# A state-space convolution beside attention on one core: the seeds' first loads, slots and powers rearranged

## The chip, the cores and the metric

The kernel runs on one core of a Trainium2 chip. A core has a matrix engine (TensorE, PE in the profile), three elementwise engines (VectorE or DVE, ScalarE or ACT, GpSimd or POOL), a queue engine that only issues transfers here (SyncE, SP) and 16 DMA engines that its queues share. The metric is the device time of one execution in microseconds; lower is better. All times below are in microseconds (us) unless marked ns.

## The reference, cut to what matters

Two independent halves are computed in float32 and put side by side. The first is a diagonal state-space layer: a kernel of 2048 taps per channel is built from 256 complex modes, and the input is convolved with it by FFT. The second is attention with 16 heads of width 28.

```python
dt = jnp.exp(log_dt)                                  # 448 channels
A = -jnp.exp(log_A_real) + 1j * A_imag                # 448 x 256 modes
C = (C_real + 1j * C_imag) * dt[:, None]
P = jnp.exp((A * dt[:, None])[:, :, None] * pos[None, None, :])   # pos = 0..2047
K = 2.0 * jnp.einsum("dn,dnl->dl", C, P).real
y = irfft(rfft(u_t, 2 * L) * rfft(K, 2 * L), 2 * L)[:, :, :L]  + u * D_skip
qkv = x @ wqkv                                        # 2048 x 448 @ 448 x 1344
p = softmax(q @ k.T * scale);  out_B = (p @ v) @ wo
```

## The kernel before, in words

The exponentials `P` are not computed one by one. For each mode only eleven powers are, those to the exponents 1, 2, 4, ... 1024 (`LV = 11`), and everything else is a product of them. The kernel has two parts in time.

**Part one** (lines 212 to 551, about the first 250 us) does two jobs side by side. `project` (line 522) works through 48 matrix products: for each of four chunks of 512 tokens, eight products that give q and k of four groups of heads (`qk_proj`) and four that give v (`v_proj`). Each product is twelve matmuls into one of three PSUM tiles `pm`. `evac` then splits the result into a high and a low part: ScalarE writes the high part `hl`, VectorE the low part, for the first two chunks ScalarE, VectorE and GpSimd also make the differences `kb` and `dhl`, and SyncE stores the tiles to DRAM. The weights are split in the same way at the start, out of tiles called `tri` that the seeds use later. A next product can run while up to two results wait for their split.

The other job is `seeds(o)` (line 313), run for eight blocks `o` of 56 channels each. Its stages are, in order: `load` (four transfers of 56 x 256 values into `nat`), `exp_a` and three products with the time step `dts`, the fourth product, `turn` (TensorE turns the four tables into one PSUM tile `pn`; ScalarE copies the real part to `tr`), `phases` (VectorE reduces the phase of one step; then eleven phases `r` are its product with the constants `pw2`; GpSimd makes the eleven real exponents `mg` as the product of `tr` with `pw2`), `reduce`, `sines` (ScalarE: two Sin and one Abs over 128 x 1232), `sizes` (ScalarE: one Exp over 128 x 1232) with `g_base`, then `places`, `factors`, `e_base`, `e3`, `g_first`, `e5`, `g_copies` (products on VectorE and GpSimd, copies on ScalarE), and last `put_g` and `put_e`, the transfers of 1456 KB and 896 KB to DRAM tensors `sd`. ScalarE holds Exp and Sin in different function tables, and a load of a table (`ACT_TABLE_LOAD`) stands between them.

The two jobs are dealt into slots (lines 504 to 540). A new seed begins every `SP = 4` slots; the 48 products are spread over `PW = 37` slots. Stage `i` of seed `o` is written in slot `4 o + i`, its load two slots ahead of the seed's first slot, so there are 41 slots. After the 37th slot the last loads of part one are written. In this part the written order is not the order of issue: a planner with its own costs orders the instructions of every engine and queue anew, from their dependencies, their place in the text and the time it expects them to be ready. A transfer also waits until the transfer eight places ahead of it in that plan has landed, since eight semaphores are used in turn.

Then come the maxima of the first query block (`max_mm(0, ...)`, lines 544 to 546): 64 matmuls, each followed by a pass of VectorE. They need `khat` (the keys of group 0, from DRAM; each quarter of its buffer holds the projection weights of one group of heads until that group's last product), `kdif`, and `qhat` (the first queries). `qhat` buffers are three, and the seeds' `se` tiles are taken from the same three.

**Part two** (from line 864) keeps the written order (`KEPT["a"]`): 256 steps of attention with the state-space work dealt between them. In the compiled programs its order on all five engines is the same before and after the change.

Of the kernel before, what the change touches and what calls it, by code (L numbers as in the profile page):

```python
# [18 lines left out]
D = 448  # L19
# [18 lines left out]
FL = {"s": 2, "f": 3}  # L38
S0, SP, SW, SD, PW, E3 = 0, 4, 0, 5, 37, 8
UG = (2, 2, 4)  # L40
# [50 lines left out]
def body(ctx, tc, a, out):  # L91
# [120 lines left out]
    with ExitStack() as st:  # L212
# [18 lines left out]
        load_x(0)  # L231
        w_g = k0_t[:CK].rearrange("p g (i s k h e) -> p i s k g h e", i=2, s=2, k=NCK, h=HG)
        vh = y_p.tile([CK, NCK, D], F32R, name="vh")
        vl = y_p.tile([CK, NCK, D], F32R, name="vl")
        nc.gpsimd.memset(k0_t[:CK].rearrange("p g (n e) -> p (g n) e", e=32)[:, :, DH:].bitcast(F32), 0.0)
        vst = [x_p.tile([128, H, 32], F32, name=f"vst{i}") for i in range(2)]
        for t in vst:
            nc.gpsimd.memset(t[:, :, DH:DH + 1], 1.0)
            nc.gpsimd.memset(t[:, :, DH + 1:], 0.0)
        wns = []  # L240
        for i in range(2):
            wn = t_p.tile([128, 3, LV, BO * 16], F32, name="tri", bufs=2).rearrange("p t k h -> p (t k h)")
            wn = wn[:CK, :2 * 3 * D].rearrange("p (k s d) -> p k s d", k=2, s=3)
            wns += [wn[:, 0], wn[:, 1]]
        for k in range(NCK):
            nc.sync.dma_start(wns[k], wqkv[k * CK:(k + 1) * CK, :].rearrange("p (s d) -> p s d", s=3))
# [5 lines left out]
        def load_nat(o):  # L252
            nats[o] = s_p.tile([PO, 4, 256], F32, name="nat", bufs=2)
            for i, n in enumerate(("A_log_A_real", "A_A_imag", "A_C_real", "A_C_imag")):
                nc.sync.dma_start(nats[o][:, i, :], bass.AP(tensor=a[n].tensor, offset=a[n].offset + first(o) * 256,
                                                            ap=[[256, JF // 4], [JF * 256, 4], [1, 256]]))

# [3 lines left out]
        for f in range(2):  # L261
            nc.sync.dma_start(ldt[4 * f:4 * f + 4, :].rearrange("o (j i) -> o j i", j=4), bass.AP(
                tensor=t.tensor, offset=t.offset + f * DF, ap=[[JF // 4, 4], [JF, 4], [1, JF // 4]]))
        load_nat(0)
        pw2 = s_p.tile([128, LV], F32, name="pw2")
        nc.sync.dma_start(pw2, a["pw2"])
        half_pi = s_p.tile([128, 1], F32, name="half_pi")
        nc.gpsimd.memset(half_pi, TWO_PI / 4)
        nc.sync.dma_start(sel, a["sel"])
        nc.sync.dma_start(w1, a["w1"])  # L270
        for k in range(NCK):
            for s in (1, 0):
                src = wns[k][:, s, :].rearrange("p (g h e) -> p g h e", g=G, e=DH)
                hi, lo = (w_g[:, i, s, k, :, :, :DH] for i in range(2))
                nc.scalar.activation(hi, src, AF.Copy)
                nc.vector.tensor_tensor(lo, src, hi.bitcast(F32), ALU.subtract)
            nc.scalar.activation(vh[:, k, :], wns[k][:, 2, :], AF.Copy)
            nc.gpsimd.tensor_tensor(vl[:, k, :], wns[k][:, 2, :], vh[:, k, :].bitcast(F32), ALU.subtract)

# [24 lines left out]
        def turn_dt():  # L304
            dt_ps = ps_t.tile([128, CQ], F32, name="pt")[:PO, :NO]
            nc.tensor.transpose(dt_ps, dt_o, ident[:NO, :NO])
            for i, f in enumerate((1.0, 0.15915494309189535, 2.0, -2.0, -1.0)):
                nc.vector.tensor_scalar(dt_all[:, i, :], dt_ps, f, None, op0=ALU.mult)

        NH = BO * 16  # L310
        mul = lambda e, o_, x_, y_: e.tensor_tensor(o_, x_, y_, ALU.mult)

        def seeds(o):
# [6 lines left out]
            vk = lambda t, k: t[:, k:k + 3, :].rearrange("p k (b h) -> p k b h", h=16)  # L320

            def exp_a():
                act.activation(q["nat"][:, 0, :], q["nat"][:, 0, :], AF.Exp)

# [4 lines left out]
            def turn():  # L329
                q["ps"] = ps = ps_n.tile([128, CQ], F32, name="pn")[:, :8 * PO].rearrange("p (a b h e) -> p a b h e", a=4, h=2, e=8)  # L330
                for i in range(4):
                    for h in range(2):
                        nc.tensor.transpose(ps[:, i, :, h, :], q["nat"][:, i, h * 128:(h + 1) * 128], ident[:PO, :PO])
                q["tr"] = s_p.tile([128, NH], F32, name="tr", bufs=2)
                act.activation(q["tr"], ps[:, 0].rearrange("p b h e -> p (b h e)"), AF.Copy)

            def phases():
                tri = t_p.tile([128, 3, LV, NH], F32, name="tri", bufs=2)
                q["r"], q["sn"], q["mg"] = r, sn, mg = tri[:, 0], tri[:, 1], tri[:, 2]
                t0, k0, im = sn[:, 0, :], sn[:, 1, :], q["ps"][:, 1].rearrange("p b h e -> p (b h e)")  # L340
                vec.tensor_scalar(k0, im, MAGIC, None, op0=ALU.add)
                vec.scalar_tensor_tensor(t0, k0, MAGIC, im, op0=ALU.subtract, op1=ALU.subtract)
                vec.tensor_scalar(t0, t0, 0.5, -0.5, op0=ALU.min, op1=ALU.max)
                mul(vec, r, lb(t0), kb)
                mul(pol, mg, lb(q["tr"]), kb)

            def reduce():
                vec.tensor_scalar(q["sn"], q["r"], MAGIC, MAGIC, op0=ALU.add, op1=ALU.subtract)
                vec.tensor_tensor(q["r"], q["sn"], q["r"], ALU.subtract)

            def sines():
                act.activation(q["sn"], q["r"], AF.Sin, scale=TWO_PI)
                act.activation(q["r"], q["r"], AF.Abs)
                act.activation(q["r"], q["r"], AF.Sin, scale=-TWO_PI, bias=half_pi)

            def sizes():
                act.activation(q["mg"], q["mg"], AF.Exp)

# [68 lines left out]
            def load():  # L427
                if o not in nats:
# [701 lines left out]
```

## Time and profile before

| | |
|---|---|
| runs (us) | 1301.16, 1301.76, 1304.81; median 1301.76 |
| profiled execution | span 1301.1 from the first to the last instruction; the page gives no other time for it |
| busy over the span | PE 94%, DVE 73%, ACT 73%, POOL 67% |
| granted TensorE clock, mean | 0.978 of full speed |
| bytes moved | 205.35 MB, 158 GB/s in the mean |

A row of the groups names line, engine, operation and tiles (`out<-in`), then how often it ran, the busy time in all, and the mean of one in ns. Nearly every instruction shows line 75, a helper that records them, so tiles tell them apart. A row of the timeline gives start, duration, engine, operation, how many were merged, and in brackets the idle time of the engine just before, with what ended it. A row of the table by stretches gives the length of the stretch, the busy time and count for each of PE, PEld (weight loads), DVE, ACT and POOL, the granted clock, the share of the DMA engines that was busy, and GB/s. SPq is the queue engine.

### The profile page before, as it was taken

How to read it: one execution, taken by the hardware profiler on the slowest of the kernel's cores; microseconds unless marked ns; L12 is line 12 of the kernel's file. 1: busy time of each engine (PE TensorE's matmuls, PEld its weight loads, DVE VectorE, ACT ScalarE, POOL GpSimd, SP SyncE). 2: the span in 40 equal slices, each digit the busy share in tenths (PEclk: the TensorE clock that was granted, in tenths of full speed). 3: DMA queues.
4: the chain of work that ended last, by engine and by line, in shares of the span. 5: the costliest groups of instructions: out<-in, count | busy, mean ns of one | idle time of the engine just before them, and what ended most of it. 6: DMA issues, size and time to landing. Idle time of an engine off the chain costs nothing.

```text
span 1301.1 us, 33177 instructions
## 1 busy us (share of the span) xinstructions
PE 1228.2 (94%) x12625; PEld 701.0 (54%) x12625; DVE 948.0 (73%) x2106; ACT 952.4 (73%) x2068; POOL 871.1 (67%) x736
## 2 busy tenths in 40 slices
PE   6878985899999999999999999999999999999997
PEld 5657763355555555555555555555555555544433
DVE  5887896987777887787788888888888655645111
ACT  4775763488888888888888888888887766756552
POOL 3676683298888878888869999998996212424421
PEclk9888997999999999999999999999999999999999
DMA  6677769835866555458644131733425453647656
GB/s 194 203 258 244 249 206 294 237 77 124 195 137 149 124 146 148 140 147 231 181 126 96 54 95 32 182 91 83 103 51 148 153 158 133 201 144 244 198 162 174
DMA packets 200088, 205.35 MB, mean 158 GB/s; under 512 B 95993, under 2 KB 158521, under 8 KB 197881
## 3 DMA queue, kind: packets, MB, share of 16 engines
q1 hardware_dynamic: 199928, 203.23, 56.2%
q8 instruction: 100, 1.64, 0.5%
q14 instruction: 60, 0.48, 0.1%
HBM read 120.73 MB, written 82.18 MB: 156 GB/s over the span
## 4 chain that ended last, share of the span: by engine, by line
PE 71%; DVE 10%; DMA 6%; POOL 5%; ACT 3%; issue 3%; SPq 0%; POOLq 0%; ACTq 0%; DVEq 0%
PE pm L75 40%; PE pss L75 16%; PE po L75 15%; DVE tri L75 2%; DVE mx L75 2%; POOL e L75 1%; POOL qhat L75 1%; DMA k<-hl 1%; ACT tri L75 1%; DVE qhat L75 1%; DVE sg L75 1%; DMA tri<-in_B_wqkv 1%; DVE px L75 1%; DMA khat<-k 1%; DMA ut<-in_A_u 1%
## 5 line engine op out<-in xcount | busy, mean ns | idle before, releaser
L75 ACT ACTIVATE p<-pss 128x512 f32<-128x512 f32 x1024 | 560.9, 609 | 111.6 <-PE pss L75 108.6
L75 PE MATMUL pss<-qhat,khat 128*128 128x512 f32 x1024 | 402.5, 399 | 1.5 <-ACT p L75 1.4
L75 DVE TENSOR_REDUCE mx<-pm 128x1 f32<-128x512 f32 x500 | 321.4, 684 | 109.2 <-PE pm L75 107.1
L75 PE MATMUL pm<-khat,qhat 128*128 128x512 f32 x749 | 326.3, 438 | 3.4 <-DVE mx L75 2.1
L75 POOL TENSOR_TENSOR e<-e,sdb 128x256 f32<-128x256 f32 x168 | 202.0, 1202 | 116.2 <-ACT e L75 61.2
L75 PE MATMUL po<-p,v 128*32 128x512 f32 x2048 | 269.1, 594 | 0.0
L75 POOL TENSOR_TENSOR e<-e,eu 128x256 f32<-128x256 f32 x168 | 248.4, 1478 | 13.2
L75 PEld LDWEIGHTS pm<-khat,qhat 128*128 128x128 f32 x749 | 141.0, 189 | 199.7 <-ACT p L75 47.8
L75 DVE CUSTOM_DVE_ANT_0 rl<-pm,rl 128x512 f32<-128x512 f32 x249 | 171.4, 688 | 65.2 <-ACT rl L75 61.5
L75 PEld LDWEIGHTS pss<-qhat,khat 128*128 128x128 f32 x1024 | 190.2, 188 | 45.7 <-issue 10.8
L75 POOL TENSOR_TENSOR eu<-e,sdb 128x256 f32<-128x256 f32 x168 | 202.2, 1203 | 0.0
L75 POOL TENSOR_TENSOR p<-pr,pr 64x448 f32<-64x448 f32 x64 | 73.3, 1145 | 158.5 <-PE pm L75 133.2
L75 ACT ACTIVATE rl<-pm 128x512 f32<-128x512 f32 x249 | 150.8, 606 | 20.4 <-PE pm L75 20.4
L75 DVE TENSOR_TENSOR g<-g,zg 128x128 f32<-128x128 f32 x392 | 162.1, 413 | 3.4
L75 PE MATMUL pm<-xh,khat 112*128 112x512 f32 x256 | 94.1, 451 | 23.2 <-DVE hl L75 11.1
L75 PE MATMUL pm<-kdif,qhat 128*128 128x512 f32 x249 | 100.5, 404 | 2.6 <-DMA v<-v 1.3
L75 DVE TENSOR_TENSOR zg<-g,zg 128x128 f32<-128x128 f32 x224 | 88.0, 393 | 5.0
L75 PEld LDWEIGHTS pm<-e,g 128*32 128x32 f32 x3584 | 57.2, 109 | 43.8 <-issue 16.1
L75 DVE TENSOR_TENSOR pr<-pm,ub 128x448 f32<-128x448 f32 x64 | 37.0, 619 | 56.4 <-PE pm L75 42.0
L75 PEld LDWEIGHTS pm<-xh,khat 112*128 112x128 f32 x256 | 54.2, 217 | 39.4 <-DVE hl L75 12.9
L75 PE MATMUL pm<-e,g 128*32 128x64 f32 x3584 | 73.0, 222 | 1.9 <-POOL e L75 1.9
L75 ACT ACTIVATE y<-pm 128x448 f32<-128x448 f32 x48 | 26.5, 553 | 58.2 <-PE pm L75 33.8
(134 smaller groups left out, 1470.3 us busy)
## 6 DMA issues: line engine op xcount, KB each, us to landing
sdb<-sd SPq DMA_DIRECT2D x56, 336.0 KB
khat<-k SPq DMA_DIRECT2D x64, 256.0 KB
qhat<-q SPq DMA_DIRECT2D x64, 256.0 KB
sd<-sg SPq DMA_DIRECT2D x8, 1456.0 KB
k<-hl SPq DMA_DIRECT2D x16, 512.0 KB
q<-hl SPq DMA_DIRECT2D x16, 512.0 KB
mw<-in_mw SPq DMA_DIRECT2D x16, 512.0 KB
sd<-qhat SPq DMA_DIRECT2D x8, 896.0 KB
```

Source lines behind the costliest of these rows:

```text
L75: i = f(*args, **kw)
```

## The change

Four things change, all in part one.

1. The first seed's parameters (`ldt`, two transfers, and `nat`, four) are written ahead of the first rows of `x` and the weights, and are issued from ScalarE's queue instead of SyncE's. `exact_exp`, the time step's exponential in small VectorE steps, is written there too; `turn_dt` moves from the second slot to the first, and `pw2` is loaded ahead of `kones`.
2. Every stage of every seed is written three slots sooner (`SH = 3`), the loads too: stage `i` of seed `o` in slot `4 o + i - 3`. There are 38 slots; the products stay spread over 37.
3. The reduced phase is written back into the PSUM tile `pn` instead of into `tri`, and VectorE's eleven-fold product reads it from there. ScalarE's copy `tr` is gone.
4. GpSimd's product for `mg` is gone, and so is the one Exp over 128 x 1232. Instead ScalarE takes eleven exponentials of 128 x 112 straight from `pn`, with the factor 2^k as its scale, in the stage of `phases`, three stages sooner than `sizes` was. A chain `in_order` ties `exp_a`, `sizes` and `sines` of all seeds to be issued on ScalarE in the order in which they are written.

```diff
-S0, SP, SW, SD, PW, E3 = 0, 4, 0, 5, 37, 8
+SP, SH, PW, E3 = 4, 3, 37, 8
...
+        def load_nat(o, queue=nc.sync):
...
+            nc.scalar.dma_start(ldt[4 * f:4 * f + 4, :].rearrange("o (j i) -> o j i", j=4), bass.AP(
+                tensor=t.tensor, offset=t.offset + f * DF, ap=[[JF // 4, 4], [JF, 4], [1, JF // 4]]))
+        load_nat(0, nc.scalar)
...
         load_x(0)
...
-        nc.sync.dma_start(kones, a["kones"])
...
-        load_nat(0)
         pw2 = s_p.tile([128, LV], F32, name="pw2")
         nc.sync.dma_start(pw2, a["pw2"])
+        nc.sync.dma_start(kones, a["kones"])
...
+        table = []
...
+            def in_order(f):
+                def call():
+                    with tc.issue_after(table[0]) if table else nullcontext():
+                        i = f()
+                    table[:] = [i.ins]
+                return call
...
-                q["tr"] = s_p.tile([128, NH], F32, name="tr", bufs=2)
-                act.activation(q["tr"], ps[:, 0].rearrange("p b h e -> p (b h e)"), AF.Copy)
...
-                t0, k0, im = sn[:, 0, :], sn[:, 1, :], q["ps"][:, 1].rearrange("p b h e -> p (b h e)")
-                vec.tensor_scalar(k0, im, MAGIC, None, op0=ALU.add)
-                vec.scalar_tensor_tensor(t0, k0, MAGIC, im, op0=ALU.subtract, op1=ALU.subtract)
+                k0, (tr, t0) = sn[:, 1, :], (q["ps"][:, i].rearrange("p b h e -> p (b h e)") for i in range(2))
+                vec.tensor_scalar(k0, t0, MAGIC, None, op0=ALU.add)
+                vec.scalar_tensor_tensor(t0, k0, MAGIC, t0, op0=ALU.subtract, op1=ALU.subtract)
                 vec.tensor_scalar(t0, t0, 0.5, -0.5, op0=ALU.min, op1=ALU.max)
                 mul(vec, r, lb(t0), kb)
-                mul(pol, mg, lb(q["tr"]), kb)
+                q["tr"] = tr
+
+            @in_order
+            def sizes():
+                return [act.activation(q["mg"][:, k, :], q["tr"], AF.Exp, scale=float(2 ** k)) for k in range(LV)][-1]
...
-            def sizes():
-                act.activation(q["mg"], q["mg"], AF.Exp)
...
-            return [[load], [exp_a] + dts(1, 2, 3), dts(0), [turn], [phases], [reduce], [sines], [sizes, g_base],
+            return [[load], [exp_a] + dts(1, 2, 3), dts(0), [turn], [phases, sizes], [reduce], [sines], [g_base],
                     [places, fa, e_base], [e3, g_first], [fb, e5, g_copies], [put_g], [put_e]]
...
-        n_stage = SP * (NO - 1) + len(stages[0])
+        n_stage = SP * (NO - 1) + len(stages[0]) - SH
...
-                slots[max(SP * o + (i or -2), 0)] += st_
-        slots[1].insert(0, turn_dt)
+                slots[max(SP * o + (i - SH if i else -2 - SH), 0)] += st_
+        slots[0].insert(1, turn_dt)
```

More of the change, by code (lines that the diff above doesn't have):

```diff
@@ L1 @@
 import collections
-from contextlib import ExitStack
+from contextlib import ExitStack, nullcontext
 import concourse.bass as bass
@@ L229, in load_x @@
                 nc.sync.dma_start(xns[c, h], xs[:, 2 * h:2 * h + 2, :])
[L231 to L246, printed above, removed]
[L247 removed]
         first = lambda o: (o // 4) * DF + (o % 4) * (JF // 4)
         nats = {}
[L252 removed]
+        def load_nat(o, queue=nc.sync):
             nats[o] = s_p.tile([PO, 4, 256], F32, name="nat", bufs=2)
             for i, n in enumerate(("A_log_A_real", "A_A_imag", "A_C_real", "A_C_imag")):
[L255 to L256 removed]
+                queue.dma_start(nats[o][:, i, :], bass.AP(tensor=a[n].tensor, offset=a[n].offset + first(o) * 256,
+                                                          ap=[[256, JF // 4], [JF * 256, 4], [1, 256]]))
         dt_all = s_p.tile([PO, 5, NO], F32, name="dt_all")
```

47 lines of the change are left out of this document (32 added, 15 removed).

## The prediction

> **What bounds the kernel now.** I read the table by stretches first, because the change touches part one alone. Part two issues in one order in both programs, so what part one saves or loses is passed on one for one, as long as part two starts from the same state.
>
> ```profile
> 0.00:200.00 200.00, 162.10 (x694) 129.06 (x695) 158.07 (x275) 136.86 (x270) 128.76 (x152) 0.91 0.69 227
> 0.00:20.00 20.00, 12.08 (x43) 9.17 (x44) 8.07 (x12) 9.26 (x17) 7.30 (x20) 1.00 0.78 214
> 80.00:100.00 20.00, 12.73 (x36) 9.79 (x37) 18.20 (x27) 17.59 (x31) 13.77 (x17) 0.68 0.65 228
> 200.00:220.00 20.00, 8.04 (x25) 5.55 (x24) 10.73 (x26) 4.03 (x9) 6.17 (x6) 0.67 1.03 296
> 220.00:240.00 20.00, 16.46 (x43) 7.45 (x43) 18.74 (x42) 6.58 (x11) 0.00 (x0) 0.99 1.05 279
> ```
>
> To be read: no engine is full in the first 200 us (TensorE 162.1, VectorE 158.1). TensorE has gaps and its granted clock falls with them (0.68 from 80 to 100, where 36 matmuls take 12.73 us). From 200 on the DMA engines are full (1.03, 1.05) and from 220 VectorE, with 18.74 of 20, makes the maxima. So part one has three limits in turn: TensorE's waits, then transfers, then VectorE. Next, TensorE's waits to 215 us:
>
> ```profile
> PE pm L75 <- DVE hl L75: 13.5, 7, 5.4
> PE pt L75 <- DMA qhat<-q: 12.0, 1, 12.0
> PE pm L75 <- DVE kb L75: 6.8, 4, 4.3
> PE pt L75 <- DVE xl L75: 6.1, 4, 2.8
> ```
>
> It waits 26.4 us for VectorE's splits (13.5 + 6.8 + 6.1) and 12.0 for the first queries. The largest wait, followed backwards from GpSimd's product for the powers:
>
> ```profile
> 77.02 3.44 POOL L75 TENSOR_TENSOR tri<-tr,pw 128x1232 f32<-128x1232 f32 x1
> ```
>
> ```profile
> 80.50 1.23 ACT L75 ACTIVATE tri<-tri 128x1232 f32<-128x1232 f32 x1 [2.79 <-POOL tri L75]
> 81.64 0.58 ACT L75 ACTIVATE hl<-pm 128x512 fp32r<-128x512 f32 x1
> ```
>
> ```profile
> 82.25 0.69 DVE L75 TENSOR_TENSOR hl<-pm,hl 128x512 fp32r<-128x512 f32 x1 [1.12 <-ACT hl L75]
> ```
>
> ```profile
> 83.00 2.08 PE L75 MATMUL pm<-xh,khat 112*128 112x512 f32 x4 [5.38 <-DVE hl L75]
> ```
>
> The Exp on ScalarE waits 2.79 us for that product. Behind it stands `hl` of a finished matrix product, behind that VectorE's half, and TensorE stands 5.38 us with all three PSUM tiles full. Its next four matmuls take 2.08. In all ScalarE waits for that product so often:
>
> ```profile
> ACT tri L75 <- POOL tri L75: 10.8, 4, 3.0
> ```
>
> The product also holds VectorE:
>
> ```profile
> 46.20 2.42 POOL L75 TENSOR_TENSOR tri<-tr,pw 128x1232 f32<-128x1232 f32 x1
> ```
>
> ```profile
> 46.92 1.77 DVE L75 TENSOR_SCALAR tri<-tri 128x112 f32<-128x112 f32 x1
> ```
>
> ```profile
> 49.35 0.47 PE L75 MATMUL pm<-vh,xh 112*128 112x448 f32 x1 [1.37 <-DVE hl L75]
> ```
>
> ```profile
> 86.52 0.22 DVE L75 TENSOR_SCALAR tri<-tri 128x112 f32<-128x112 f32 x1
> 86.77 1.44 DVE L75 TENSOR_TENSOR tri<-tri,pw 128x1232 f32<-128x1232 f32 x1
> ```
>
> A 128 x 112 operation that takes 0.22 alone took 1.77 and ended with GpSimd's product (46.20 + 2.42 = 48.62, 46.92 + 1.77 = 48.69). VectorE's split came after it, and TensorE lost 1.37. VectorE's own eleven-fold product took 1.44 where GpSimd was idle.
>
> The end of part one is a queue of transfers:
>
> ```profile
> 199.90 1.61 SPq L75 DMA_DIRECT2D qhat<-q  x2
> 202.10 0.50 SPq L75 DMA_DIRECT2D sd<-sg  x1
> 214.87 0.77 PE L75 MATMUL pt<-kdif,qhat 128*128 128x512 f32 x1 [11.96 <-DMA qhat<-q]
> ```
>
> ```profile
> sd<-sg SPq DMA_DIRECT2D x8, 1456.0 KB
> ```
>
> TensorE has been done for 11.96 us when the queries arrive. Between the two halves of their load stands a 1456 KB transfer of the seventh seed.
>
> **The change, part by part.** The durations:
>
> ```profile
> L75 ACT ACTIVATE tri<-tri 128x1232 f32<-128x1232 f32 x24 | 29.6, 1234 | 15.7 <-POOL tri L75 10.8 <-DVE tri L75 4.8
> ...
> L75 POOL TENSOR_TENSOR tri<-tr,pw 128x1232 f32<-128x1232 f32 x8 | 19.4, 2419 | 14.3 <-ACT tr L75 8.5 <-issue 5.8
> L75 ACT ACT_TABLE_LOAD x15 | 19.2, 1283 | 1.0 <-PEq L1120 0.7
> ...
> L75 DVE TENSOR_TENSOR tri<-tri,pw 128x1232 f32<-128x1232 f32 x8 | 15.1, 1886 | 0.1
> ...
> L75 DVE TENSOR_SCALAR tri<-tri 128x112 f32<-128x112 f32 x8 | 8.0, 1003 | 0.1
> ...
> L75 ACT ACTIVATE tr<-pn 128x112 f32<-128x112 f32 x8 | 2.2, 271 | 1.1 <-PE pn L75 0.9
> ```
>
> *Powers.* GpSimd loses 8 products of 2.419, 19.4 us. ScalarE loses 8 Exp of 1.234 and 8 copies of 0.271, and gets 88 exponentials of 128 x 112. One alone should take the 0.271 of the copy, which has the same source and shape; in a row they overlap:
>
> ```profile
> 195.35 1.22 ACT L75 ACTIVATE sg<-sg 128x112 f32<-128x112 f32 x6
> ```
>
> Six take 1.22, or 0.2 each, so eleven take 0.27 + 10 x 0.2 = 2.3 (at most 11 x 0.271 = 3.0). ScalarE pays 8 x (2.3 - 1.23 - 0.27) = +6.4, at most +12. The tied order makes 17 table loads of 15: two times 1.283 is +2.6. Together +9, and the 10.8 us of waits for GpSimd go: ScalarE is about even. The page "ScalarE: Activation LUTs" of the Trainium skill (section "What ACT_TABLE_LOAD costs") speaks against this: a switch of tables should cost about 2.66, a load of 1.283 and a drain of 1.38. By that rule the two loads would cost 5.3 and ScalarE's sum would be +11.7. The trace does not agree:
>
> ```profile
> 36.50 1.28 ACT L75 ACT_TABLE_LOAD   x1
> 37.79 1.23 ACT L75 ACTIVATE tri<-tri 128x1232 f32<-128x1232 f32 x1
> ```
>
> The Sin starts 0.01 after the load's end (36.50 + 1.28 = 37.78), so I keep 1.283 and +9.
>
> On the path: the waits of TensorE that follow from GpSimd's product are 5.38 and 1.37. I count both as gone, -6.75. The slow clock behind the larger comes on top. At the full clock two matmuls take 0.63:
>
> ```profile
> 36.91 0.63 PE L75 MATMUL pm<-xh,khat 112*128 112x512 f32 x2
> ```
>
> The 36 matmuls from 80 to 100 would then take 11.3 (18 x 0.63) and not 12.73: -1.4. What is late next at that place is VectorE's own `reduce`, also ahead of the split. The last of ScalarE's waits for GpSimd falls among the transfers of the end and is not counted twice.
>
> *Phases in PSUM.* The 128 x 112 step should take about 0.27 instead of 1.003, and cannot be held as above: -5.9 on VectorE. The eleven-fold product is bounded by 1.886 (no gain) and 1.44 (never held), -3.6. The page "SBUF — State Buffer" of the Trainium skill ("Who interferes with whom") says that two SBUF inputs, or a two-port mode, make VectorE and GpSimd exclude each other, and one input from PSUM does not. By that rule all 3.6 would come; the held and the free row above agree, but no run yet has the PSUM form. Of these 5.9 to 9.5 us little is on TensorE's path; its 12.9 us of waits for `kb` and `xl` come from VectorE's backlog. VectorE was busy 158.1 of the first 200 us, so a relief of 8 is a twentieth; I take twice that share of 12.9, -1.3, with 0 and half of it, -6.5, as ends.
>
> *Parameters first.* Six transfers move to ScalarE's queue and their 229 KB ahead of the weights.
>
> ```profile
> 1.20 0.93 SPq L75 DMA_DIRECT2D xn<-in_B_x  x2
> 2.17 1.94 SPq L75 DMA_DIRECT2D tri<-in_B_wqkv  x4
> ...
> 4.73 0.77 SPq L75 DMA_DIRECT2D ldt<-in_A_log_dt  x2
> 6.23 1.02 SPq L75 DMA_DIRECT2D nat<-in_A_log_A_real  x1
> ```
>
> ```profile
> 0.73 1.28 ACT L75 ACT_TABLE_LOAD   x1 [0.73 <-PEq L1120]
> 6.97 0.60 ACT L75 ACTIVATE xh<-pt 112x512 fp32r<-112x512 f32 x1 [4.96 <-PE pt L75]
> ```
>
> The issue costs 0.77 for `ldt` and about 1.0 for each of four `nat`, so about 4.8 us on ScalarE ahead of its table load: 0.73 + 4.8 + 1.28 = 6.8, and its first split was at 6.97 after 4.96 of idle time. That gap hides it; without it, it would cost the 4.8. On SyncE the weights' four issues now wait for `ldt`, the first rows of `x` and one `nat` to land, through the eight semaphores in turn (`nat` at 6.23 shows such a wait). Transfers of `x` are under way until then, so I charge only the bytes: 229 KB at 214 GB/s is +1.1; at worst nothing is under way and the weights start at 6.97, when the first rows have been turned, instead of 2.17: +4.8. The time step's small VectorE operations now fall in the idle start; TensorE's listed waits name none of them, so 0.
>
> *Three slots sooner.* By the plans, the seeds' order against the products moves by about two products at the end (the last Sin stood behind three of the last eight `hl`, and stands behind two). All later stages of a seed move, with their four loads and two `put` transfers on SyncE. No work goes. The seventh seed's 1456 KB now stand ahead of the first `khat` load, and the sixth seed's 2352 KB no longer fall among the last eight products: 1456 KB fewer are moved between the start of those products and the queries. At the 296 GB/s of the row from 200 to 220 that is 1456 / 296 = -4.9. If the transfers ahead have not drained, 0. The eighth seed's `put_g` still comes before three quarters of `khat`; these are needed one after another, and the maxima (VectorE 18.74 of 20 from 220) cover them.
>
> *New order.* The seeds' work now presses on ScalarE and VectorE sooner, and eleven exponentials stand in a block ahead of a split, where one Exp of 1.23 stood. Two of the three PSUM tiles cover a block of 2.3; where all are full it costs 2.3. I charge one such block, +2.3 (none to all eight, 18.4).
>
> Sum: -6.75 - 1.4 - 1.3 + 1.1 - 4.9 + 2.3 = -11.0. The span becomes 1301.1 - 11.0 = 1290.1; the median of the runs lies 0.7 above the span, so 1290.8.
>
> **The rivals.**
>
> *Slower: ScalarE's tied order.* Each seed's Sin must now wait for the next seed's `exp_a` and for its own eleven exponentials, and every split behind them waits too. For it: ScalarE is busy 17.59 of 20 us from 80 to 100, the stretch with the worst clock. Against it: the waits for GpSimd that it replaces are as long. Without the charge the sum is -13.3, so it decides from the sixth block of 2.3 on that meets full PSUM tiles: with all eight, +18.4 instead of +2.3, the sum is +5.1, and the time 1306.9.
>
> *No change at the end.* The transfers, full from 200 us, set when the queries arrive, and TensorE's gain turns into a longer wait for them (11.96 now). For it: shares of 1.03 and 1.05. Against it: SyncE had room before, with a share of 0.65 from 80 to 100. Then the gains ahead of it and the -4.9 vanish; with +1.1 the time is 1302.9.
>
> *More than the forecast.* The waits for `kb` and `xl` (12.9) are also offspring of GpSimd's product, and the clock stays up. For it: VectorE's rows held by it. Then half of 12.9 goes (-6.5 in place of -1.3) and no block is charged: -11.0 - 5.2 - 2.3 = -18.5, and 1283.3.
>
> **How the numbers follow.** Within 0.3% (3.9 us) of 1301.8 is about what a measurement cannot tell from no change. Forecast (1286 to 1297): 0.45. More: 0.20. No change at the end: 0.13, of which 0.04 keeps a gain of over 3.9. ScalarE's order: 0.19, of which 0.04 ends within 0.3%. The rest, 0.03, is a start that loses its 4.8 with no gain behind it. Faster: 0.45 + 0.20 + 0.04 = 0.69; same: 0.09 + 0.04 = 0.13; slower: 0.15 + 0.03 = 0.18. The range of eight in ten goes from 1280, beyond the third rival, to 1307, the first; the forecast's own range is 1286 to 1297.
>
> **What would show it.** ScalarE has no wait for GpSimd at `tri`, the eleven exponentials take 2.3 a block, table loads are 17; the 128 x 112 step on `pn` takes under 0.3 and the product on `pn` about 1.44; the largest wait of TensorE for `hl` is under 3; the queries arrive about 11 us sooner, and maxima and part two follow unchanged. Wrong it would be if waits of ScalarE for VectorE's `phases` took the place of those for GpSimd, or if TensorE ended sooner and the queries did not.

## The result, and the profile after

The changed kernel takes 1295.20 us (median of 1294.08 to 1295.62) against 1303.28 (1301.16 to 1305.12) for the kernel before on the same chip: a ratio of 0.993, with an interval of 0.9912 to 0.9948. It is 8.1 us faster; 11.0 were forecast. Its profiled execution took 1295.62, with a span of 1293.7 (before 1301.1).

The table by stretches of the changed kernel (length, then PE, PEld, DVE, ACT and POOL busy, granted clock, share of the DMA engines, GB/s):

```profile
0.00:20.00 20.00, 11.95 (x40) 8.66 (x41) 11.49 (x38) 10.86 (x22) 6.76 (x20) 1.00 0.87 237
...
80.00:100.00 20.00, 12.70 (x44) 9.69 (x43) 17.84 (x35) 16.74 (x41) 14.27 (x19) 0.83 0.72 249
...
200.00:220.00 20.00, 12.16 (x31) 6.66 (x31) 13.15 (x29) 5.56 (x10) 0.00 (x0) 0.71 1.05 288
220.00:240.00 20.00, 15.27 (x37) 7.60 (x38) 18.23 (x41) 5.46 (x10) 0.00 (x0) 0.89 0.81 214
0.00:200.00 200.00, 162.01 (x705) 127.77 (x705) 143.79 (x288) 142.17 (x348) 109.12 (x150) 0.94 0.74 245
```

Over 200 us VectorE does 143.79 instead of 158.07, GpSimd 109.12 instead of 128.76, ScalarE 142.17 instead of 136.86. From 80 to 100 the clock is 0.83 and no longer 0.68. From 200 to 220 the DMA engines are as full as before (1.05 for 1.03), from 220 to 240 they are less so (0.81 for 1.05). TensorE's waits up to 235 us:

```profile
PE pt L75 <- DMA khat<-k: 12.6, 1, 12.6
PE pm L75 <- DVE kb L75: 11.0, 5, 3.7
PE pm L75 <- DVE hl L75: 6.7, 5, 1.8
...
PE pt L75 <- DVE xl L75: 2.7, 2, 2.4
```

The waits for `hl` have halved (13.5 before), those for `xl` have more than halved (6.1), but those for `kb` have grown from 6.8 to 11.0. The wait of the maxima's first matmul is still there: 12.6, was 12.0, now put down to the keys (`khat`) and no longer to the queries. The groups of ScalarE and VectorE up to 215 us, and one block of exponentials in the timeline:

```profile
L75 ACT ACT_TABLE_LOAD x17 | 21.8, 1283 | 10.0 <-issue 5.1 <-DVE tri L75 4.7
...
L75 ACT ACTIVATE tri<-pn 128x112 f32<-128x112 f32 x88 | 15.1, 311 | 1.6 <-DVE tri L75 1.5
```

```profile
L75 DVE TENSOR_TENSOR tri<-pn,pw 128x1232 f32<-128x1232 f32 x8 | 11.4, 1430 | 0.0
...
L75 DVE TENSOR_SCALAR pn<-pn 128x112 f32<-128x112 f32 x8 | 2.3, 283 | 0.1
```

```profile
84.94 1.28 ACT L75 ACT_TABLE_LOAD   x1
86.23 1.83 ACT L75 ACTIVATE tri<-pn 128x112 f32<-128x112 f32 x11
```

A block of eleven takes 1.83, the table loads are 17, and no wait of ScalarE for GpSimd at `tri` is left. The end of part one, on the queue engine and then on TensorE:

```profile
190.95 2.53 SPq L75 DMA_DIRECT2D khat<-k  x4
...
194.33 1.45 SPq L75 DMA_DIRECT2D qhat<-q  x2
195.90 0.49 SPq L75 DMA_DIRECT2D q<-hl  x1
196.43 1.10 SPq L75 DMA_DIRECT2D qhat<-q  x2
```

```profile
206.56 0.76 PE L75 MATMUL pt<-kdif,qhat 128*128 128x512 f32 x1 [12.63 <-DMA khat<-k]
```

The row of the kernel before that answers to the first of these:

```profile
196.57 1.80 SPq L75 DMA_DIRECT2D khat<-k  x4
```

The load of the first keys is issued 5.6 us sooner (190.95 for 196.57), and from that issue to the maxima's first matmul 15.6 us pass instead of 18.3 (206.56 - 190.95; 214.87 - 196.57). Together that is 8.3, and from there to the end both kernels take about the same: 1293.7 - 206.56 = 1087.1 and 1301.1 - 214.87 = 1086.2. So the whole gain is made before the maxima.

### The profile page after: what moved, and what is told of

It is laid out like the page before. It is cut to its first block, busy times and chain, and to the rows that moved or that the text cites. A ratio compares the mean times of both kernels' runs of the same rounds, so it can differ in the third digit from the quotient of the medians.

```text
span 1293.7 us, 33256 instructions
## 1 busy us (share of the span) xinstructions
PE 1226.7 (95%) x12625; PEld 699.1 (54%) x12625; DVE 928.4 (72%) x2106; ACT 956.2 (74%) x2142; POOL 844.5 (65%) x728
## 3 DMA queue, kind: packets, MB, share of 16 engines
q8 instruction: 100, 1.64, 0.5%
## 4 chain that ended last, share of the span: by engine, by line
PE 76%; DVE 9%; POOL 4%; DMA 4%; ACT 3%; issue 3%; SPq 0%; ACTq 0%; POOLq 0%; DVEq 0%
PE pm L75 43%; PE pss L75 17%; PE po L75 16%; DVE mx L75 2%; POOL qhat L75 2%; DVE rl L75 1%; DMA khat<-k 1%; DMA sd<-qhat 1%; DVE tri L75 1%; ACT tri L75 1%; DVE qhat L75 1%; DVE sg L75 1%; DVE px L75 1%; POOL x_e L75 1%; POOL p L75 1%
## 5 line engine op out<-in xcount | busy, mean ns | idle before, releaser
L75 POOL TENSOR_TENSOR eu<-e,sdb 128x256 f32<-128x256 f32 x168 | 202.0, 1202 | 0.0
L75 ACT ACTIVATE rl<-pm 128x512 f32<-128x512 f32 x249 | 151.3, 607 | 20.2 <-PE pm L75 20.1
L75 PE MATMUL pm<-xh,khat 112*128 112x512 f32 x256 | 89.4, 436 | 19.7 <-DVE kb L75 10.5
```

Source lines behind the costliest of these rows:

```text
L75: i = f(*args, **kw)
```

## A measure for part one: idle time and half clock

Three rows of tables by stretches, each from the start to the end of the last of the 48 products: the kernel before, the changed kernel, and the change without its second part (told of below).

```profile
0.00:202.91 202.91, 165.01 (x705) 131.08 (x705) 160.52 (x281) 136.86 (x270) 130.30 (x154) 0.91 0.69 227
```

```profile
0.00:193.93 193.93, 162.01 (x705) 127.77 (x705) 143.79 (x288) 142.17 (x348) 109.12 (x150) 0.94 0.74 245
```

```profile
0.00:183.25 183.25, 153.47 (x705) 121.47 (x705) 141.87 (x281) 140.93 (x344) 105.95 (x146) 0.98 0.75 250
```

The same 705 matmuls are 165.0, 162.0 and 153.5 us of busy time, because the granted clock differs (0.91, 0.94, 0.98). In stretches of a few microseconds it is almost always 1.00 or 0.50. I add up, over stretches of 1 us, busy time times (1 - clock): that is what half clock cost. What is left of the busy time is 149.0 to 151.3 us in every kernel below. So the end of the products is about 150 us, plus TensorE's idle time, plus that loss. The columns: median time and ratio to the kernel before in the same comparison; end of the last product, idle time and loss to half clock up to there; time from the issue of the first keys to the maxima; their start (us, profiled execution).

| kernel | time | ratio (interval) | products end | idle | half clock | keys to maxima | maxima |
|---|---|---|---|---|---|---|---|
| before | 1303.28 | | 202.9 | 37.9 | 15.7 | 18.3 | 214.9 |
| the change | 1295.20 | 0.9930 (0.9912-0.9948) | 193.9 | 31.9 | 11.2 | 15.6 | 206.6 |
| powers and phases alone | 1292.20 | 0.9916 (0.9902-0.9931) | 192.1 | 31.1 | 11.5 | 18.7 | 204.0 |
| loads and slots alone | 1304.51 | 1.0011 (1.0001-1.0021) | 203.6 | 41.7 | 11.7 | 16.3 | 214.2 |
| change without slots | 1287.40 | 0.9882 (0.9866-0.9898) | 183.3 | 29.8 | 3.4 | 18.5 | 196.1 |
| change without parameters first | 1292.97 | 0.9926 (0.9913-0.9939) | 193.4 | 31.4 | 12.3 | 15.6 | 204.8 |
| phases in PSUM alone | 1305.05 | 1.0008 (0.9998-1.0018) | 200.4 | 38.0 | 11.3 | 18.6 | 214.9 |
| powers alone | 1295.29 | 0.9943 (0.9928-0.9958) | 193.7 | 32.1 | 10.4 | 18.4 | 206.5 |
| change, one slot sooner | 1295.28 | 0.9937 (0.9924-0.9949) | 189.7 | 30.9 | 9.4 | 21.5 | 206.3 |
| without slots, 1456 KB late | 1284.81 | 0.9862 (0.9841-0.9882) | 185.8 | 29.1 | 5.7 | 14.7 | 194.5 |
| powers and phases, dead product | 1291.77 | 0.9920 (0.9907-0.9934) | 192.0 | 30.9 | 11.2 | 18.2 | 202.1 |
| 1456 KB late, queries sooner | 1288.20 | 0.9889 (0.9872-0.9906) | 194.8 | 33.4 | 11.2 | 18.5 | 194.6 |
| without slots, free order | 1290.18 | 0.9907 (0.9892-0.9922) | 188.9 | 27.2 | 12.7 | 18.7 | 202.0 |

The kernel before had medians of 1302.49 to 1303.90 in the four comparisons. A planner orders every variant anew, so a difference of 2 or 3 us between two of them can be a single wait that appeared or not. And each row but for the time and the ratio is one execution. The last experiment's kernel issues part one in the same order as the change without slots, on all engines, and so is a second execution of it: there the products end at 185.5, half clock costs 5.0, and the maxima start at 198.5 (183.3, 3.4 and 196.1 in the table). Two microseconds in those columns can be chance.

## The experiments

**Powers and phases alone.** The first parameters are loaded after the weights on SyncE, `exact_exp` follows the weights' splits, and no slot moves.

```diff
-SP, SH, PW, E3 = 4, 3, 37, 8
+SP, SH, PW, E3 = 4, 0, 37, 8
...
-        load_nat(0, nc.scalar)
+        load_nat(0)
```

> The powers and the phases alone (parts 3 and 4 of the change): the first parameters are loaded where they were, and no stage is moved in the slots. Powers theory (the product of GpSimd that held ScalarE and VectorE was most of the loss): 6 to 8 us faster than before (-6.75 for the two waits of TensorE, -1.4 for the clock, -1.3 for VectorE, +2.3 for one block of exponentials), and the wait of 5.38 is gone. Slots theory (most of the gain is made within the last eight products, where the traces differ by 6.3 us, because stages of the seeds have left them): only the 2.7 us that the changed kernel had won before these products, so 1 to 3 us faster.

Measured: 10.6 us faster, 1292.2. By the medians that is more than the whole change (8.1), though the two intervals overlap. The waits of 5.38 and 1.37, ahead of the eighteenth and the eleventh product, are gone. But ahead of the twentieth, where the kernel before waited 4.27 for `kb`, TensorE now waits 4.61 for `hl`, since ScalarE's split waits for a store:

```profile
81.60 0.60 ACT L75 ACTIVATE hl<-pm 128x512 fp32r<-128x512 f32 x1 [3.42 <-DMA q<-hl]
```

```profile
82.97 0.74 PE L75 MATMUL pm<-vh,xh 112*128 112x448 f32 x1 [4.61 <-DVE hl L75]
```

In all the waits for `hl` are 13.1 (13.5 before); what fell are those for `kb` (3.6 for 6.8) and for `xl` (3.4 for 6.1). TensorE's idle time is 6.8 us shorter and half clock costs 4.2 less.

**Loads and slots alone.** GpSimd's product, the copy `tr`, the one Exp and the phases in SBUF are put back, parts 1 and 2 stay.

> Parts 1 and 2 alone: parameters first and every stage three slots sooner, with the product of GpSimd, the copy and the one Exp as before. Powers theory: within 1 us of before, on the slow side by the 1.1 us of the parameters, since the 4.9 us hoped for at the queries were not seen; ScalarE still waits about 11 us for GpSimd. Slots theory: 5 to 7 us faster, made within the last eight products.

Measured: 1304.5, a ratio of 1.0011. ScalarE still waits for GpSimd (7.7 us in 4 times), TensorE's idle time is even longer than before (41.7). The powers theory holds; the slots theory, which the place of the gain in the traces had suggested, falls.

**The change without the slots** (`SH = 0` alone).

> The whole change without the three slots (SH = 0): parts 1, 3 and 4. Powers theory: 5 to 7 us faster than before, that is 1 to 3 us slower than the whole change. Slots theory: 0 to 2 us faster than before, about 6 us slower than the whole change.

Measured: 1287.4, 15.4 us faster than before. Both theories miss it, and on the same side: the three slots do not help, they cost 6 to 8 us here (7.8 by the medians, 6.3 by the ratios). The table says where: the products end 10.7 us sooner, 7.8 of that from half clock (3.4 for 11.2) and 2.1 from idle time. (This profile is of the fastest of its executions, 1285.47, so the difference of the two profiles is larger than that of the medians; against the second execution it is 8.4 us, 6.2 of them half clock and 2.0 idle time.) One place shows what half clock does. The changed kernel, a wait and the stretches behind it:

```profile
39.66 0.73 PE L75 MATMUL pm<-xh,khat 112*128 112x512 f32 x2 [2.13 <-DVE kb L75]
```

```profile
42.00:45.00 3.00, 3.00 (x9) 2.37 (x8) 2.81 (x9) 3.00 (x11) 2.40 (x4) 0.50 0.30 96
45.00:48.00 3.00, 3.00 (x9) 2.61 (x9) 3.00 (x5) 1.36 (x2) 0.42 (x2) 0.53 0.72 243
```

The kernel without the slots, a wait of nearly the same length:

```profile
45.32 0.47 PE L75 MATMUL pm<-vh,xh 112*128 112x448 f32 x1 [2.17 <-DVE kb L75]
```

```profile
45.00:48.00 3.00, 2.68 (x13) 2.52 (x14) 3.00 (x10) 1.93 (x8) 2.84 (x4) 1.00 0.72 260
48.00:51.00 3.00, 3.00 (x17) 2.81 (x16) 3.00 (x5) 2.61 (x5) 1.25 (x2) 1.00 0.29 97
```

After 2.13 us of waiting TensorE had half clock from about 42 to 48 us and did 9 matmuls in each 3 us; after 2.17 us, in the other kernel, it kept the full clock and did 13 to 17. The last experiment shows why two waits of one length can differ so. It does not come from the two orders alone: in the second execution of the kernel without slots the clock was at half from 38.5 to 41.9 us, in the first it was full there.

**The change without parameters first.** Part 1 undone, slots three sooner.

> The whole change without its first part: the first seed's parameters are loaded after the weights on the queue engine, as before, while the stages stay three slots sooner. If the parameters first cost the 1.1 us that the start of the changed trace shows (first split at 8.19 and not 6.97), this is 1 us faster than the whole change, about 9 us faster than before. Rival: the first seed now comes too late for its earlier slots, TensorE waits in order for the turned tables, and it is 2 us or more slower than the whole change.

Measured: 1293.0, against 1295.2 with parameters first; by the ratios only 0.5 us are between them (0.9926 and 0.9930), so there is no difference that could be told, and the rival falls. With the slots where they were there is one, in the same comparison and the other way: 1287.4 with parameters first, 1292.2 without. So it does more than the 1.2 us that it costs at the start. Without it (powers and phases alone), VectorE's time-step chain stands in the second and third product, and the first seed is turned behind it; with it (change without slots) the first seed is turned 9 us sooner:

```profile
21.05 0.17 DVE L75 TENSOR_SCALAR x<-ldt 8x56 f32<-8x56 f32 x1
...
27.11 0.20 DVE L75 COPY dt_o<-dt 8x56 f32<-8x56 f32 x1
...
30.08 0.71 PE L75 MATMUL pn<-ident,nat 56*128 56x56 f32 x8
```

```profile
21.14 0.70 PE L75 MATMUL pn<-ident,nat 56*128 56x56 f32 x8
```

The third product's split comes at 25.04 instead of 29.54. Three slots sooner takes that gain away again: the split is then at 28.56, and the thirteenth product's at 71.07 (61.28 without the slots), since the seeds' work of three slots stands ahead of the first products. That this turn of the first seed is what the 4.8 us come from is not shown: by the table most of the difference is half clock (11.5 for 3.4, or 5.0 in the second execution), and the transfers, the chain and the turn of `dt` moved together.

The four kernels with the new powers and phases show that the other two parts act on each other: 1292.2 with neither, 1287.4 with parameters first, 1293.0 with the slots, 1295.2 with both. So the slots cost 6 to 8 us only beside parameters first; without them it is 0.8 us, which the intervals do not tell from nothing. Without parameters first, too, they delay the thirteenth product (73.70 for 60.00), but by the forty-fourth most of that is made good (184.46 for 181.10).

**Phases in PSUM alone.**

> Part 3 alone: the reduced phase stays in PSUM; GpSimd's product, the copy on ScalarE, the loads and the slots are as before. Prediction's term: -1.3 us (ends 0 and -6.5); the 128 x 112 step falls from 1.0 to under 0.3, the eleven-fold product from 1.89 to about 1.44, and ScalarE still waits some 11 us for GpSimd. Rival (VectorE's relief was the gain of the powers and the phases together): most of the 10.6 us that both together brought, so 6 to 10 us faster.

Measured: 1305.1, a ratio of 1.0008: nothing. Its waits and groups:

```profile
ACT tri L75 <- POOL tri L75: 9.0, 3, 4.1
```

```profile
L75 POOL TENSOR_TENSOR tri<-tr,pw 128x1232 f32<-128x1232 f32 x8 | 18.0, 2250 | 10.5 <-issue 5.8 <-ACT tr L75 4.6
...
L75 DVE TENSOR_TENSOR tri<-pn,pw 128x1232 f32<-128x1232 f32 x8 | 11.5, 1434 | 0.2
```

The two instructions are as short as forecast, with GpSimd's product still running, and it gains nothing. In the next kernel, with phases in SBUF and no product on GpSimd, the step takes 0.239 and the eleven-fold product 1.506: for VectorE, PSUM and the absence of GpSimd do nearly the same.

**Powers alone** (eleven exponentials in the tied order; the phase goes to SBUF as before).

> Part 4 alone: eleven exponentials on ScalarE in the tied order, without GpSimd's product; the phase goes to SBUF as before, loads and slots are as before. If the waits for GpSimd's product were the loss, this brings most of the 10.6 us of parts 3 and 4 together: 8 to 10 us faster. If the prediction's sizes hold, 6 us (-6.75 - 1.4 + 2.3). Rival: what remains after VectorE's relief is taken away, 0 to 4 us.

Measured: 1295.3, 8.6 us faster by the medians, 7.4 by the ratio (5.5 to 9.4 by its interval). It makes most of the 10.6. What the phases add on top (about 3 us) is within what the two intervals leave open.

**One slot sooner** (`SH = 1`).

> The whole change with the stages one slot sooner (SH = 1) instead of three; with none the time was 1287.4, with three 1295.2. If the earlier seeds cost TensorE evenly, a third of the 7.8 us: about 1290. Rival (the cost is made of single waits of TensorE just over 2 us, each of which also halves its clock for some microseconds, and which a shift makes or unmakes as it happens): a step, the time lies within 1.5 us of one of the ends or beyond them, and the time at half clock before the last product follows it, near 3 us for 1287 and near 12 us for 1295.

Measured: 1295.3, the time of three slots: not an even cost. The rival is right in kind only in part. Half clock cost 9.4 us, not 12, and the products end at 189.7, 4.2 us ahead of the change. But the maxima start no sooner, because here two of the seeds' transfers stand ahead of the second half of the queries:

```profile
184.74 2.15 SPq L75 DMA_DIRECT2D khat<-k  x4
...
187.42 0.46 SPq L75 DMA_DIRECT2D sd<-sg  x1
187.93 2.34 SPq L75 DMA_DIRECT2D qhat<-q  x2
...
191.80 0.39 SPq L75 DMA_DIRECT2D sd<-qhat  x1
192.24 4.26 SPq L75 DMA_DIRECT2D qhat<-q  x2
```

From the first keys to the maxima 21.5 us pass. With neither transfer in between it is 14.7 to 16.3, with the 1456 KB 18.2 to 18.7 (queries sooner left aside, where the maxima follow the last product).

**The 1456 KB late** (without slots; `late` holds the seventh seed's `put_g` and is written after `load_v`).

```diff
-            for f in slots[t] + ahead.get(t, []):
+            for f in [f for f in slots[t] if f not in late] + ahead.get(t, []):
                 f()
```

> The whole change without the slots (SH = 0, 1287.4), and with the seventh seed's 1456 KB written to DRAM only after the loads of the maxima; nothing else moves by more than the queue engine's order. If the transfers ahead of the queries set the start of the maxima, as the prediction's -4.9 had it, the maxima start 5 us sooner and the time is about 1282.5. Rival (the transfers ahead of it have not drained, or the issue of the loads is what is late): within 1 us of 1287.4.

Measured: 1284.8, the fastest kernel of all, 2.6 us less than without the edit (1287.4; the two were not compared side by side).

```profile
179.75 1.77 SPq L75 DMA_DIRECT2D khat<-k  x4
...
182.05 1.60 SPq L75 DMA_DIRECT2D qhat<-q  x2
183.76 0.46 SPq L75 DMA_DIRECT2D q<-hl  x1
184.58 0.88 SPq L75 DMA_DIRECT2D qhat<-q  x2
```

```profile
194.49 0.77 PE L75 MATMUL pt<-kdif,qhat 128*128 128x512 f32 x1 [8.65 <-DMA qhat<-q]
```

From the first keys to the maxima 14.7 us instead of 18.5: the transfer was worth 3.8. The products ended 2.6 us later, 2.3 of it half clock, so 1.6 arrive at the maxima. Against the second execution of the order without the edit the products end nearly alike (185.8 for 185.5), and 4.0 arrive.

**Dead product.** Powers and phases alone, with GpSimd's product for nothing.

```diff
+                q["tr_s"] = s_p.tile([128, NH], F32, name="tr", bufs=1)
+                act.activation(q["tr_s"], ps[:, 0].rearrange("p b h e -> p (b h e)"), AF.Copy)
...
+                dead = s_p.tile([128, 8, NH], F32, name="dead")
+                for i, j in ((0, 8), (8, LV)):
+                    mul(pol, dead[:, :j - i], lb(q["tr_s"])[:, i:j], kb[:, i:j])
```

> The powers and phases alone (the kernel that was 10.6 us faster), with GpSimd's eleven-fold product and ScalarE's copy for it kept as dead work: the product is made as before (in two pieces of 8 and 3 powers), but nothing reads it, and the exponentials still come from PSUM. If ScalarE's wait for the product was the loss, at least 8 of the 10.6 us stay. If the load on GpSimd and its hold on VectorE were the loss, 3 us or less stay.

Measured: 1291.8, 10.7 us faster than before. GpSimd does 20.1 us of dead work and the copies are back on ScalarE:

```profile
L75 POOL TENSOR_TENSOR dead<-tr,pw 128x896 f32<-128x896 f32 x8 | 13.9, 1738 | 5.8 <-ACT tr L75 5.8
...
L75 POOL TENSOR_TENSOR dead<-tr,pw 128x336 f32<-128x336 f32 x8 | 6.2, 770 | 0.5
```

All of the gain stays. The load on GpSimd cost nothing that shows; that ScalarE stood and waited for it, with the splits behind, was the loss. (VectorE's step cannot be held by the product in either of the two kernels, since the phases are in PSUM; but that alone gained nothing.)

**Queries sooner.** The kernel with 1456 KB late, `A1` 34 to 32 and `KW` (33, 35, 36) to (32, 34, 36).

> A try for a faster kernel: the whole change without the slots, the seventh seed's 1456 KB after the loads of the maxima (1284.8 so far), and the loads of the queries two slots and of the first two key quarters one slot sooner, so that both halves of the queries stand ahead of the first keys. Then only 1024 KB of keys lie between their issue and the maxima, instead of the keys, 1536 KB of queries and new q and k: the 14.7 us between them shrink to 7 to 9 and the maxima start about 6 us sooner, 1279 to 1281. Rival (the same bytes are needed anyway, the maxima then wait for the second quarter): 1284 to 1286.

Measured: 1288.2, a miss. The wait of the maxima is gone altogether: they follow the last product at once, at 194.57. But the products end at 194.8 instead of 185.8. Of that, 2.7 us stand already at a wait of 4.1 that both kernels have (its end is at 180.65 for 177.95); behind it comes one that was not there, followed by half clock:

```profile
189.28 1.22 PE L75 MATMUL pm<-xh,khat 112*128 112x512 f32 x2 [4.03 <-DVE hl L75]
```

Ahead of it, ScalarE's copies of the last seed waited 3.94 us for VectorE with a split behind them. And from the maxima to the end it takes longer, 1286.0 - 194.6 = 1091.4 for 1087.0; the wait for the second quarter of the keys, which the rival named, is not among TensorE's waits. The end of part one is held from two sides: who closes one gap meets the other.

**Free order** (without slots; `in_order` ties nothing).

> The whole change without the slots (1287.4) and without the tied order of ScalarE's exponentials and sines. If the tied order costs something (the prediction's slower rival), this is 2 us or more faster. If it saves what it was charged with, the switches of tables: more than 17 table loads of 1.28 before the queries and 2 us or more slower. Within 1 us if the planner makes nearly that order by itself.

Measured: 1290.2, some 2.8 us slower than with the tie (ratios 0.9907 and 0.9882, whose intervals overlap), with the same number of table loads:

```profile
L75 ACT ACT_TABLE_LOAD x17 | 21.8, 1283 | 7.9 <-issue 5.2 <-DVE tri L75 2.6
```

So the tied order costs nothing; whether it gains is not settled, since 12.7 us of half clock for 3.4 would explain more than the difference.

**The cost of a gap by itself.** The kernel without slots, with this behind its end:

```diff
+    for n in 2 * (512, 3000, 1000, 1750, 4000, 1500, 2500, 750, 2250, 1250, 3500, 2000):
+        nc.scalar.activation(rt[:, :n], src[:, :n], AF.Copy)
+        for _ in range(40):
+            nc.tensor.matmul(pb, rt[:, :128], rt[:, :CQ], start=True, stop=True)
```

> The cost of a gap by itself: behind the end of the same kernel (its output is unchanged) stand 24 times 40 matmuls of 128 x 512; before each group TensorE waits for one copy on ScalarE over 512 to 4000 columns, so that gaps of about 0.8 to 4.3 us are made, each length twice. Theory: no gap under 2 us lowers the granted clock, every gap over 3.4 us does, those between do or don't; the lowered clock is 0.50 and lasts 3 to 7 us, so a gap over the bound costs 1.5 to 3.5 us more than its length. Rival: the clock falls by degrees with the share of idle time, short gaps included.

Three groups of 40 matmuls, with the wait ahead of each in brackets:

```profile
1300.62 10.99 PE L75 MATMUL pb<-gap 128*128 128x512 f32 x40 [2.85 <-ACT gap L75]
...
1323.97 10.98 PE L75 MATMUL pb<-gap 128*128 128x512 f32 x40 [1.81 <-ACT gap L75]
```

```profile
1351.23 9.38 PE L75 MATMUL pb<-gap 128*128 128x512 f32 x40 [1.60 <-ACT gap L75]
```

Leaving out the first group, which follows a long pause: all 9 groups after waits of 0.78 to 1.60 took 9.36 to 9.38; of 8 after 1.81 to 2.44, six took 10.91 to 10.99 (2.02 gave 9.37 once and 10.95 once); all 6 after 2.85 to 3.69 were slow, five by 1.5 to 1.6 and one by 2.8. So the cost is a step and not a slope, and its lower bound lies below the 2 us that I had expected. The section "Part 1" of the page "TensorE: Matmul & The Clock Gate" in the Trainium skill says that the clock is either half or full, and that about 3.4 us of sustained work bring it back; the loss of 1.6, half of 3.2, agrees. Its rule that idle gaps over about 3.4 us are the harmful ones (section "HAM oscillation") does not agree: 1.81 did it twice.

In the products themselves it is the same with less sharp bounds. Of 104 waits of 1 us and more in twelve of the traces (all but queries sooner and this one), after 20 us and ahead of the last product: none of 16 up to 1.37 had the clock at half within 2 us of its end, 28 of 55 between 1.38 and 2.56 had, and all 33 longer ones.

What decides between the two bounds can be read from the places of the waits. Two more groups followed waits of the same length, 2.44 us: one started at 1363.04 and took 10.91, one started at 1510.33 and took 9.38. For each, the stretch of 3.41 us in which its wait begins, and the next:

```profile
1359.48:1362.89 3.41, 1.13 (x5) 1.00 0.00 0
1362.89:1366.30 3.41, 3.26 (x8) 0.50 0.00 0
1506.25:1509.66 3.41, 1.64 (x8) 1.00 0.00 0
1509.66:1513.07 3.41, 2.74 (x12) 1.00 0.00 0
```

The granted clock changes only at the edges of such stretches: in every trace the times of its changes lie on one grid of 3.41 us (in the kernel before 56.49, 63.32, 80.38 and 87.21, for instance), and the grid lies differently from one execution to another. The slow group's wait falls almost whole into one stretch, idle for 3.41 - 1.13 = 2.28; the other is divided, 1.77 and 0.67. In this part of the run, of 71 stretches at full clock all 12 that were idle for 1.81 or more were followed by half clock, and none of the 59 idle for 1.77 or less. In the products of all fourteen traces, from 20 us on, there are 600 such stretches: none of the 510 idle for less than 1.37 was, 8 of the 30 up to 1.64 were, and all 60 above that. So the two waits of 2.13 and 2.17 differ by their places: the first lay whole in the stretch from 37.55, the second was divided at 43.69, into 0.54 and 1.63.

## Why the prediction was right, and where it was wrong

The sign was right, and 1295.2 lies in the forecast's own range. The sum was right for a partly wrong reason: without the slots' term it was -6.1, and that kernel (change without slots) measured -15.4; the slots, counted as -4.9, cost 6 to 8 us beside it. These are two errors of opposite sign, and that they nearly cancel is luck. A small one comes on top: the 0.7 between span and time compares two executions; every execution on record lies 1.8 to 2.3 us above its own span (1295.62 for 1293.7).

- *Powers*: the cause was right, and the dead product shows it: ScalarE's wait and not GpSimd's load. For the powers alone -6.75 - 1.4 + 2.3 = -5.85 was forecast, and they brought -8.6 by the medians, with the forecast just inside the interval of 5.5 to 9.4; with the phases it was -7.15 for a measured -10.6, outside it (9.0 to 12.8). With both, idle time fell by 6.8, as the -6.75 had it, and the two waits that it named are gone, though by the sums others for `hl` took their place and those for `kb` and `xl` shrank. (In the changed kernel the eighteenth product still waits 3.65, at 84.53, now for `kb`.) The term that was too small is the clock's: -1.4 for a measured -4.2 (15.7 to 11.5). It took 0.63 as the full clock's time for two matmuls, but matmuls overlap: the next one starts 0.47 later (36.91, 37.38), so that 36 would take about 8.5 (18 x 0.47), and by the measure above the stretch from 80 to 100 lost 4.6 to half clock. ScalarE's price was too high: 88 exponentials take 15.1, so 15.1 - 8 x 1.234 - 2.2 = +3.0 instead of +6.4. The table loads are 17, as said, and the next instruction starts 0.01 after the load (84.94 + 1.28 = 86.22, 86.23). Ahead of the 15 loads of the kernel before, ScalarE was idle for 1.0 us in all. The measurement stays against the drain of the page "ScalarE: Activation LUTs" in the Trainium skill (section "What ACT_TABLE_LOAD costs").
- *Phases in PSUM*: the durations were right (0.28 and 1.43), the term of -1.3 was not found: alone it measures +1.1, no difference.
- *Parameters first*: the start costs what the +1.1 had it: the first split of the weights, which waits for its transfer, comes at 10.61 for 9.38, and in the mean of all traces 1.1 later with parameters first (10.6 in eight, 9.5 in six). ScalarE's issues took 5.1 in the gap that was to hide them. (The first split of `x`, at 8.19 for 6.97, stands behind the first seed's exponential and is no measure: in the two executions of one order it came at 8.45 and 6.76.) The step that failed is the sentence that charged 0 for moving the time step's chain. Part 1 ends the turn of the first seed 9 us sooner and is worth 4.8 us where the slots are not moved; where they are, no gain can be told.
- *Three slots sooner*: the step that failed is "No work goes", with only transfers charged. The transfers came, at 2.7 instead of 4.9 (18.3 to 15.6), and in the two pairs of kernels that differ in the slots alone the maxima follow the first keys 2.9 and 3.1 us sooner. But in both the products end later, by 1.3 us (without parameters first) and by 10.7 (with them), since work that moves ahead of the first products delays them. At the split of the thirteenth product the change stands 9.8 us behind the kernel without slots (71.07 for 61.28), at that of the forty-fourth 12.5 (185.91 for 173.40); in the pair without parameters first the delay was mostly made good. Most of the loss is half clock (11.2 for 3.4, or 5.0 in the second execution); which waits lose the clock is not something the plan of slots lets one foresee.
- *New order*: no block of exponentials showed up as 2.3 us on the path; waits for `hl` fell. What grew are the waits for `kb`.
- *The rivals*: ScalarE's tied order costs nothing that was found (free order is not faster). That the transfers decide the end is half true: they set about 15 to 18 us from the first keys to the maxima, but these follow the products, so that a gain ahead is passed on. The change without its second part (1287.4) lies between the forecast (1290.8) and "more than the forecast" (1283.3), still in the forecast's own range.

Of the signs that were named, the table loads (17), the step and the product on `pn` and the largest wait for `hl` (1.8) came as said; a block took 1.83 and not 2.3, and the maxima start 8.3 us sooner and not 11.

What stays open: why the slots cost so much beside parameters first and next to nothing without; whether the loss through moved slots would be as large under another order of the same work, since each variant was ordered anew, and what the phases in PSUM add once the powers are changed.

## What to carry to other kernels

A producer that is busy is not the trouble; a consumer that waits for it in an in-order queue, with others' work behind it, is. Look for the wait whose followers are on the path, and take the dependence away rather than the load. When work is moved sooner, ask what it stands ahead of, and cost that delay even where no work is added. Change one part at a time: here the best kernel (1284.8) is the change without its second part, with one transfer put later.

## What the runs showed of the hardware

A wait of TensorE has two prices. The first is its length. The second is half clock for 3.41 us or a multiple of that, 1.5 to 1.6 us lost in a dense stream, once 2.8. Up to 1.37 us no wait had the second price, from 2.58 us on every wait had; in between it depends on the wait's place on a grid of 3.41 us. In the stream of matmuls made for it, 1.81 us of idle time or more within one stretch of the grid always brought half clock, 1.77 or less never; in the products the bound lies between 1.37 and 1.64. Since the grid lies differently from one execution to another, one order can lose different amounts (3.4 and 5.0 us in the two executions of the kernel without slots).

In part one of the kernel before this second price was 15.7 us, two fifths of the idle time itself (37.9). Of the 19.6 us by which the change without slots ends its products sooner (202.9 for 183.3), 12.3 are half clock; by its second execution it is 10.7 of 17.4.
